# Fused retention and gated feed-forward kernel: the four sums of X move from GpSimd to VectorE, and half of a weight tile is reloaded by two transfers

## Chip, cores and metric

The kernel runs on one core of one Trainium2 chip. The metric is device microseconds of one execution. Time before: median 659.03 us of three runs (656.14 to 660.89).

## What is computed

```python
def _attn_ref(q, k, v):                      # q, k, v: (4, 8, 768, 64) float32
    gamma = 1.0 - 2.0 ** (-5.0 - np.arange(H))
    for t in range(S):
        state = gamma * state + np.einsum('bhd,bhe->bhde', k[:, :, t], v[:, :, t])
        y[:, :, t] = scale * np.einsum('bhd,bhde->bhe', q[:, :, t], state)
...
def _moe_ref(x, w_in, w_out):                # w_in: 512 x 2048, w_out: 2048 x 512
    h = x @ w_in
    g = h * (1.0 / (1.0 + np.exp(-1.702 * h)))
    return g @ w_out
...
    x = attn_out.transpose(0, 2, 1, 3).reshape(B * S, H * D)   # 3072 x 512
```

A recurrence over 768 positions (32 pairs of batch and head) makes X, 3072 rows of 512. X goes through a matrix, a gate and a second matrix.

## The kernel before

The 3072 rows are worked in six blocks of 512 tokens, m = 0 to 5. For each block there is an up part (X times the first matrix, then the gate, into the tile G) and a down part (G times the second matrix, then the output). The retention of the next block (one chunk of 64 positions for two batches at a time, called a step) is interleaved with the down part, so that X of block m+1 is complete when block m's down part is nearly over. Blocks 2 to 5 use a seven-product scheme for both parts: sums and differences of quadrants of the operands are made first, and each 2 by 2 block product then takes seven products instead of eight.

TensorE's order is the program's order. The other engines' orders are decided by a scheduler at build time, except for instructions pinned with `tc.keep_in_program_order`. Each engine works its queue in order: an instruction that waits holds all behind it.

**Sums of X.** The up part of a block reads X as seven pieces. X[:, 0] to X[:, 3] are the quadrants, and `sums_x` (L529 to L533) makes X[:, 4], X[:, 6], X[:, 5] and finally a new X[:, 2] by four subtractions of 128x512 float32 on GpSimd. It is called once a block, in the down part of blocks 1 to 4, after the unit of work that also takes the last retention step (L1025, L1026). Of the four only the first is pinned. `step` (L375) ends with `output` (L338), whose last write of X is the VectorE addition at L352.

**The up part** (`up`, L558) does four groups d, in the order 2, 3, 0, 1 for blocks 3 to 5. In each group the products come in the order P1 (weights in W1A, X[:, 0]), P2 (W1A, X[:, 1]), P6 (weights in LATE, X[:, 5]), P5 (LATE, X[:, 4]), P7 (LATE, X[:, 6]), then P3 and P4 (W1A, X[:, 3] and X[:, 2]). P1, P6, P7 and P4 add up in one PSUM tile, `px`; P2 is in `py`. A product of a group is eight matmuls of 128x256 and about 1.73 us.

**LATE** holds 48 columns of 128 weights per partition. LATE[:, 0:24] serves groups d = 0 and 1, LATE[:, 24:36] serves d = 2 and LATE[:, 36:48] serves d = 3. In the down part the tile is a workspace: `stream` (L651) loads pieces of the second matrix into one quarter and `derive` (L662) has VectorE write sums of G into another. So the weights are reloaded from a copy in HBM, W1D, once a block: ScalarE's queue issues the reload of LATE[:, 24:48] at L766, GpSimd's queue that of LATE[:, 0:24] at L999.

**The down part** (`down49`, L657) has seven products i, each in two halves, so 14 units. L766 stands behind unit i = 5, half 1, the last reader of LATE[:, 24:48]. In blocks 2 to 4 the units of i = 6 follow, whose two halves are in the PSUM tiles `pq` with the tag "x". ScalarE copies each half out (L701, `put`). The first `px` of the next up part takes over the PSUM buffer of the first half, so that TensorE's first matmul of the up part waits for the first of these two copies. Behind them in ScalarE's queue is the copy of P1 out of `px` (L573), which P6 waits for.

**Loads.** SP's queue brings q, k and v for the steps ahead: per step eight transfers each for `q_sq` and `k_sq` (L163), four for `kn_in` and four for `v_in` (L149). As the program is built, every transfer issued from SP's and ScalarE's queues signals its landing on one of eight semaphores, taken in turn; a transfer waits, before it is issued, for the landing of the one that had the same semaphore before it, also where that belongs to the other queue. In block 2 the reload at L766 waits in this way for the third `kn_in` transfer of the step, besides its true dependences (TensorE's last reads, VectorE's L670, an earlier stream and the copy in W1D).

Of the kernel before, what the change touches and what calls it, by code (L numbers as in the profile page):

```python
# [28 lines left out]
def kernel(  # L29
# [29 lines left out]
    pe, act, dve, pool, sp = nc.tensor, nc.scalar, nc.vector, nc.gpsimd, nc.sync  # L59
# [21 lines left out]
    late = ctx.enter_context(tc.tile_pool(name="late", bufs=1))  # L81
# [9 lines left out]
    LATE = late.tile([P, 2 * NP * 3, P], F32, name="LATE")  # L91
    W1L = LATE.rearrange("p (n s c) f -> p n s c f", s=3, c=2)
    W1D = [dram.tile([P, NP * 3, P], F32, name=f"W1D{i}") for i in range(2)]
# [3 lines left out]
    X = const.tile([P, 7, 2, TH], F32, name="X")  # L97
# [428 lines left out]
        pool.tensor_sub(w[5], w[4], w[0])  # L526
        pool.tensor_sub(w[2], w[1], w[5])

    def sums_x():  # L529
        tc.keep_in_program_order(pool.tensor_sub(X[:, 4], X[:, 2], X[:, 0]))  # L530
        pool.tensor_sub(X[:, 6], X[:, 3], X[:, 2])
        pool.tensor_sub(X[:, 5], X[:, 3], X[:, 4])
        pool.tensor_sub(X[:, 2], X[:, 1], X[:, 5])  # L533
# [7 lines left out]
    def sums_w2_t3(p):  # L541
        dve.tensor_sub(W2[:, 6, p:p + 2, :], W2[:, 5, p:p + 2, :], W2[:, 0, p:p + 2, :])
# [92 lines left out]
    def inner_w2_t3(i):  # L635

        b11, b12, b21, b22 = w2q(ORDER[i][1])
        tc.keep_in_program_order(dve.tensor_sub(b12, b22, b12))
# [12 lines left out]
    def stream(i, engine=pool):  # L651

        c = LATE[:, i % 2 * 24:i % 2 * 24 + 12].rearrange("p (k d) e -> p k d e", k=3)
        engine.dma_start(c, W2D[i])  # L654
        return c

    def down49(m, comps):  # L657

        b, t0 = m * CB // NC * 2, m * CB % NC * D
# [4 lines left out]
        def derive(i):  # L664
            q = [G[:, u::2, ORDER[i][0], h * P:(h + 1) * P] for u in range(2) for h in range(2)]
            a11, s3, a12, s2 = q
            d = LATE[:, i % 2 * 24 + 12:i % 2 * 24 + 24].rearrange("p (k d) e -> p k d e", k=3)
            dve.tensor_add(d[:, 0], s2, a11)
            dve.tensor_sub(d[:, 1], a12, s2)
            dve.tensor_add(d[:, 2], s2, s3)  # L670
            b11, t3, b21, b22 = w2q(ORDER[i][1])
            t1, t2, t4 = [comps[i][:, k] for k in range(3)]
            return [(a11, b11), (a12, b21), (s2, t2), (s3, t3)], [(d[:, 0], t1), (d[:, 1], b22), (d[:, 2], t4)]

        def products(p0, pairs, new):
            for j in ((0, 1, 3, 2) if len(pairs) == 4 else range(len(pairs))):
                a, w = pairs[j]
                for d in range(NP // 2):
                    pe.matmul(p0[:, j, :], a[:, d], w[:, d], start=(new and j == 0 and d == 0),  # L679
                              stop=(d == NP // 2 - 1), skip_group_check=True)  # L680
# [33 lines left out]
        def then(i, half, p0):  # L714
            if i == 0:
                act.activation(acc["y", half], p0, AF.Copy)
            elif i == 1:
                put(0, 0, half, p0, None)
            elif i == 2:
                act.activation(keep("u", half), p0, AF.Copy)  # L720
            elif i == 3:
                act.activation(keep("v", half), p0, AF.Copy)
            elif i == 4:
                put(1, 1, half, p0, "v")
            elif i == 5:
                put(0, 1, half, p0, "u")
            else:
                put(1, 0, half, p0, "v" if m == NB - 1 else None)

        def finish(p0, ab):  # L730

            c, v = kept[1, 0], kept["v"][1]
            p1 = ps.tile([P, 2, P], F32, name="pq", tag="x")
            products(p0, ab[:1], True)
            products(p1, ab[1:], True)
            at = [rows[1, 0][:, b, f * P:(f + 1) * P] for b in range(2) for f in range(2)]
            dve.tensor_add(c[:, 1:3], c[:, 1:3], c[:, 0:1].to_broadcast([P, 2, P]))
            act.dma_start(at[0], c[:, 1])
            dve.tensor_add(c[:, 3], c[:, 3], c[:, 2])
            dve.tensor_add(c[:, 4], p0[:, 0], v[:, 0])  # L740
            dve.tensor_add(c[:, 0:5:4], c[:, 2:4], c[:, 4:5].to_broadcast([P, 2, P]))
            act.dma_start(at[3], c[:, 4])
            dve.tensor_add(c[:, 5:7], c[:, 0:4:3], v[:, 1:3])
            dve.tensor_add(c[:, 2:4], p1, c[:, 5:7])
            for n in range(2):
                (act, sp)[n].dma_start(at[1 + n], c[:, 2 + n])
# [3 lines left out]
        for i in range(7):  # L750
            for half in range(2):
                def unit(i=i, half=half):
                    if half == 0:
                        if i == 0:
                            pairs[0] = derive(0)
                        for x in {0: "xy", 4: "y", 6: "y" if m == NB - 1 else ""}.get(i, ""):
                            for n in range(2):
                                acc[x, n] = ps.tile([P, 4 - n, P], F32, name="pq", tag=x)
                    x = "x" if i in (0, 2, 3) or (i == 6 and m < NB - 1) else "y"
                    if i == 6 and half == 1 and m == NB - 1:  # L760
                        finish(acc[x, half], pairs[i][half])
                        return
                    products(acc[x, half], pairs[i][half], i in (0, 4) or (i == 6 and m == NB - 1))
                    then(i, half, acc[x, half])
                    if i == 5 and half == 1 and m < NB - 1:
                        act.dma_start(LATE[:, 24:48], W1D[1])  # L766
                    if half == 0 and i < 6:
                        pairs[i + 1] = derive(i + 1)
                    if half == 1:
                        if i + 2 < 7:  # L770
                            comps[i + 2] = stream(i + 2)
                        if i in (0, 1, 3):
                            sums_g_outer((0, 1, None, 2)[i])
                todo.append(unit)
# [206 lines left out]
    for m in range(NB):  # L981
        between = []
        if m == 0:
            between = [lambda: None, lambda: None, lambda: turn(2 * CB), lambda: step(2 * CB), lambda: None,
                       lambda: turn(2 * CB + 1)]
        elif m == 1:
            between = [lambda: (decay(2 * CB), load(2 * CB + 1, "v"))]
            for j in range(2 * CB + 1, 3 * CB + 1):
                between.append(lambda j=j: (step(j, j - 1), j < 3 * CB and turn(j + 1)))
        elif 1 < m < NB - 1:  # L990
            last = min((m + 2) * CB, NCH - 1)
            for j in range((m + 1) * CB + 1, last + 1):
                between.append(lambda j=j: (step(j, j - 1), j < last and turn(j + 1)))
            if last == NCH - 1:
                between.append(lambda: step(None, NCH - 1))
        if m > 1:
            ds = (0, 1, 2, 3) if m == 2 else (2, 3, 0, 1)
            if m > 2:
                pool.dma_start(LATE[:, 0:24], W1D[0])  # L999
            for n, d in enumerate(ds):  # L1000
                up(d, ds[n - 1] if n else None, ds[n + 1] if n < 3 else None)
                if m == 2 and n < 2:
                    tc.keep_in_program_order(sp.dma_start(W1D[n], LATE[:, 24 * n:24 * n + 24]))
                if n == 0 and m < NB - 1:
                    turn((m + 1) * CB + 1)
                if d == 0:
                    comps = {0: stream(0)}
                if n == 2:
                    comps[1] = stream(1)
                if m == 2:  # L1010
                    for i in range(2 * d, min(7, 2 * d + 2)):
                        inner_w2_t3(i)
        for n, unit in enumerate(down(m) if m < 2 else down49(m, comps)):
            unit()
            if m == 0 and n < NP and n % 2:
                sums_w2(n - 1)
            if m == 0 and NP <= n < 3 * NP // 2:
                sums_w2_t3(2 * (n - NP))
            if m == 1 and n % 8 == 3:
                sums_w1(n // 4)  # L1020
            if (m, n) in INNER:
                inner_w2(INNER.index((m, n)))
            if between and (n in (2, 5, 11, 16, 21) if m == 1 else n % 3 == (1 if m else 2)):
                between.pop(0)()
            if 0 < m < NB - 1 and n == (23 if m == 1 else 11):  # L1025
                sums_x()  # L1026


# [44 lines left out]
```

## Time and profile before

| | before |
|---|---|
| median of three runs | 659.03 us |
| span of the profiled execution | 659.4 us |
| TensorE matmul busy | 639.5 us (97%) |
| VectorE busy | 427.4 us (65%) |
| ScalarE busy | 165.2 us (25%) |
| GpSimd busy | 195.7 us (30%) |
| mean granted TensorE clock | 0.995 |
| LATE<-W1D from ScalarE's queue, 1536 KB, issue to landing | 7.6 us median of 3 |
| LATE<-W2D from GpSimd's queue, 768 KB, issue to landing | 5.0 us median of 28 |
| one subtraction of `sums_x` on GpSimd | 1.27 to 1.28 us |

The profiled execution is one run of the program with the hardware profiler on; no time other than its span is given for it, and the span is 0.4 us above the median of the unprofiled runs. Times in the trace are microseconds from the start of that span. "SPq", "ACTq" and "POOLq" are the queues of SyncE, ScalarE and GpSimd, q1 is the set of DMA rings that SP issues on, q10 those of ScalarE, q0 those of GpSimd. PE is TensorE's matmul, PEld its weight load, DVE is VectorE, ACT is ScalarE and POOL is GpSimd. An idle time is named with what ended it. Block 2's up part runs from 259 to 308 us, its down part to 360; block 3's from 360 to 410 and 462; block 4's from 462 to 512 and 564; block 5 ends the program.

### The profile page before, as it was taken

The numbers are of one execution on the slowest core, as the hardware profiler recorded it, in microseconds if no ns is written. First come the engines' busy times: TensorE is split into PE (matmuls) and PEld (weight loads), VectorE is DVE, ScalarE is ACT, GpSimd is POOL, SyncE is SP. The second block draws the span as 40 slices with busy tenths as digits, with TensorE's granted clock in tenths as the row PEclk, the third lists the DMA queues.
The fourth block names the chain that finished last, engine by engine and source line by source line (L and its number), as shares of the span: only waits on it lengthen the run. The fifth ranks groups of instructions, "written<-read, shape, count | busy, mean of one in ns | idle before, by whom it ended". The sixth has DMA issues, their size and how long they took to land.

```text
span 659.4 us, 15196 instructions
## 1 busy us (share of the span) xinstructions
PE 639.5 (97%) x6390; PEld 577.1 (88%) x6390; DVE 427.4 (65%) x599; ACT 165.2 (25%) x320; POOL 195.7 (30%) x222
## 2 busy tenths in 40 slices
PE   6789999999999999999999999999999999999997
PEld 3678888888788888889999888999888999888997
DVE  3699989999936963348883336984145984144855
ACT  4674334551000000333101323100333210233210
POOL 6400321210478218000727400535500335500000
PEclk9799999999999999999999999999999999999999
DMA  9996649763243456550577821486741244601142
GB/s 174 185 274 186 175 89 246 188 139 54 48 96 144 120 155 160 183 169 1 157 161 213 224 50 49 124 192 175 235 79 49 71 141 145 237 2 49 52 157 97
DMA packets 148149, 89.77 MB, mean 136 GB/s; under 512 B 131600, under 2 KB 134416, under 8 KB 147056
## 3 DMA queue, kind: packets, MB, share of 16 engines
q1 hardware_dynamic: 135856, 44.66, 30.2%
q0 software_dynamic: 9456, 38.16, 18.5%
q10 hardware_dynamic: 2768, 5.96, 2.6%
q8 instruction: 50, 0.82, 0.5%
q14 instruction: 19, 0.16, 0.1%
HBM read 71.32 MB, written 14.94 MB: 131 GB/s over the span
## 4 chain that ended last, share of the span: by engine, by line
PE 83%; DMA 8%; DVE 4%; SPq 2%; POOL 1%; issue 1%; ACT 0%; DVEq 0%; ACTq 0%; POOLq 0%
PE pq L679 22%; PE px L564 16%; PE pd L814 13%; PE pz L564 8%; PE ph L417 8%; PE ph L492 7%; PE py L564 4%; DMA W<-in_moe_w_in_dram 2%; PE pa L294 2%; DMA LATE<-W1D 1%; DMA G<-in_moe_w_in_dram 1%; PE py L317 1%; PE py L311 1%; PE pa L302 1%; DMA kn_in<-in_k_dram 1%; SPq L146 1%
## 5 line engine op out<-in xcount | busy, mean ns | idle before, releaser
L654 POOL DMA_DIRECT2D LATE<-W2D x28 | 15.5, 555 | 236.4 <-PE pq L679 125.0
L679 PE MATMUL pq<-W,G 128*128 128x128 f32 x672 | 80.2, 276 | 0.0
L679 PEld LDWEIGHTS pq<-W,G 128*128 128x128 f32 x672 | 77.6, 192 | 0.6
L564 PE MATMUL px<-X,LATE 128*128 128x256 f32 x256 | 60.7, 380 | 2.2 <-DMA LATE<-W1D 1.2
L564 PE MATMUL px<-X,W1A 128*128 128x256 f32 x256 | 60.5, 379 | 0.0
L679 PE MATMUL pq<-LATE 128*128 128x128 f32 x448 | 59.8, 276 | 0.0
L417 PE MATMUL ph<-X,W1A 128*128 128x256 f32 x256 | 57.4, 382 | 1.6 <-DVE X L352 1.1
L564 PEld LDWEIGHTS px<-X,LATE 128*128 128x128 f32 x256 | 48.5, 190 | 9.5 <-issue 1.5
L417 PEld LDWEIGHTS ph<-X,W1A 128*128 128x128 f32 x256 | 48.0, 190 | 8.5 <-DVE X L352 1.2
L679 PEld LDWEIGHTS pq<-LATE 128*128 128x128 f32 x448 | 54.5, 192 | 0.4
L564 PEld LDWEIGHTS px<-X,W1A 128*128 128x128 f32 x256 | 48.4, 190 | 6.5
L814 PE MATMUL pd<-W,G 128*128 128x256 f32 x224 | 49.6, 381 | 0.0
L814 PEld LDWEIGHTS pd<-W,G 128*128 128x128 f32 x224 | 42.2, 190 | 5.8
L599 DVE TENSOR_TENSOR G<-pz,vv 128x512 f32<-128x512 f32 x16 | 11.1, 692 | 49.3 <-ACT vv L579 49.3
L398 ACT ACTIVATE G<-G 128x512 f32<-128x512 f32 x48 | 29.8, 628 | 44.4 <-DVE G L607 22.2
L814 PE MATMUL pd<-W,LATE 128*128 128x256 f32 x160 | 35.8, 382 | 1.2 <-DVE LATE L548 1.2
L814 PEld LDWEIGHTS pd<-W,LATE 128*128 128x128 f32 x160 | 30.1, 190 | 6.2 <-DVE LATE L548 2.2
L701 ACT ACTIVATE o<-pq 128x512 f32<-128x512 f32 (+1 forms) x14 | 7.6, 544 | 90.8 <-PE pq L679 90.8
L564 PE MATMUL pz<-X,W1A 128*128 128x256 f32 x128 | 30.3, 379 | 0.0
L564 PE MATMUL py<-X,W1A 128*128 128x256 f32 x128 | 30.2, 379 | 0.0
L564 PE MATMUL pz<-X,LATE 128*128 128x256 f32 x128 | 30.2, 379 | 0.0
L679 PE MATMUL pq<-LATE,G 128*128 128x128 f32 x224 | 29.6, 275 | 0.0
(206 smaller groups left out, 1175.3 us busy)
## 6 DMA issues: line engine op xcount, KB each, us to landing
LATE<-W2D POOLq DMA_DIRECT2D x28, 768.0 KB, 5.0
W<-in_moe_w_in_dram SPq DMA_DIRECT2D x12, 512.0 KB, 4.8
W<-in_moe_w_out_dram SPq DMA_DIRECT2D x10, 512.0 KB, 5.0
out_dram<-o POOLq DMA_DIRECT2D x20, 256.0 KB, 3.8
q_sq<-in_q_dram SPq DMA_DIRECT2D x144, 32.0 KB, 2.5
k_sq<-in_k_dram SPq DMA_DIRECT2D x144, 32.0 KB, 2.2
v_in<-in_v_dram SPq DMA_DIRECT2D x72, 64.0 KB, 3.0
LATE<-W1D ACTq DMA_DIRECT2D x3, 1536.0 KB, 7.6
```

The lines of the kernel that those rows point to most:

```text
L146: keep(engine.dma_start(*((to, at) if name == "v" else (to[:, n:H:2], at[:, n * HP:(n + 1) * HP]))))
L294: pe.matmul(pa[HALF[w], u, 0, s, :], kt[HALF[u], w, s, :], qt[HALF[u], w, s, :], start=True, stop=True)
L302: pe.matmul(pa[HALF[u], w, 1, s, :], kd[HALF[w], HP * u + s, :], vn[HALF[w], HP * u + s, :], start=True, stop=True)
L398: pin(act.activation(g, h[:, i], AF.Gelu_apprx_sigmoid))
L417: pe.matmul(h[:, ab], w, X[:, 2 * th + c // 2, c % 2, :], start=(ab == 0 and c == 0), stop=(c == 3), skip_group_check=True)
L492: pe.matmul(acc[:, u, :], w, x, start=(start and u == 0 and c == 0), stop=(stop and c == 1), skip_group_check=True)
L564: pe.matmul(acc[:, u, :], w1(2 * d + u, sw)[:, c, :], X[:, sx, c, :], start=(start and u == 0 and c == 0), stop=(stop and c == 1), skip_gr ...
L599: dve.tensor_add(a[3], z, v)
L654: engine.dma_start(c, W2D[i])
L679: pe.matmul(p0[:, j, :], a[:, d], w[:, d], start=(new and j == 0 and d == 0), stop=(d == NP // 2 - 1), skip_group_check=True)
L701: act.activation(to, y, AF.Copy)
L814: pe.matmul(p0[:, n, :], g1(m, p, sa)[:, n * P:(n + 1) * P], W2[:, sb, p, :], start=(new and p == 0 and n == 0), stop=(last and p == NP - ...
```

## The change

For blocks 2 to 4 (`m > 1`) the four subtractions are done by VectorE, in the order X[:, 4], X[:, 5], X[:, 6], X[:, 2], all four pinned. In VectorE's order as built they stand behind the last step's L352 and the copy-out of unit i = 5 (L703), and ahead of the first addition of the next up part (L588). Block 1 keeps GpSimd. The reload of LATE[:, 24:48] becomes two transfers, of LATE[:, 24:36] and of LATE[:, 36:48], both from ScalarE's queue at the same place. TensorE's order does not change; lines after the edits are 4 or 5 higher in the changed kernel.

```diff
-    def sums_x():
+    def sums_x(late):
+        if late:
+            for to, a, b in ((4, 2, 0), (5, 3, 4), (6, 3, 2), (2, 1, 5)):
+                tc.keep_in_program_order(dve.tensor_sub(X[:, to], X[:, a], X[:, b]))
+            return
         tc.keep_in_program_order(pool.tensor_sub(X[:, 4], X[:, 2], X[:, 0]))
         pool.tensor_sub(X[:, 6], X[:, 3], X[:, 2])
         pool.tensor_sub(X[:, 5], X[:, 3], X[:, 4])
...
                     if i == 5 and half == 1 and m < NB - 1:
-                        act.dma_start(LATE[:, 24:48], W1D[1])
+                        for a in range(2):
+                            act.dma_start(LATE[:, 24 + 12 * a:36 + 12 * a], W1D[1][:, 12 * a:12 * a + 12])
...
             if 0 < m < NB - 1 and n == (23 if m == 1 else 11):
-                sums_x()
+                sums_x(m > 1)
```

## The prediction

> **What bounds the kernel now.** I read the page's busy times and chain of waits first, then who TensorE waits for, then the timeline at the three places that the change touches: the passages from a down part to the next up part near 360, 462 and 564 us.
>
> ```profile
> PE 639.5 (97%) x6390; PEld 577.1 (88%) x6390; DVE 427.4 (65%) x599; ACT 165.2 (25%) x320; POOL 195.7 (30%) x222
> ```
>
> The first line is busy us, share and instructions of each engine; the next two are TensorE's waits, with the total, the count and the longest in us.
>
> ```profile
> PE px L564 <- DMA LATE<-W1D: 1.2, 1, 1.2
> PE px L564 <- POOL X L532: 1.0, 1, 1.0
> ```
>
> TensorE is busy 97% of the span, so only what it waits for can pay, and the change can remove two of these waits, one each. The third passage (564 us) has no wait at all. The first passage, block 2 to 3, in the timeline (start, duration, engine, line):
>
> ```profile
> 355.19 2.57 SPq L149 DMA_DIRECT2D v_in<-in_v_dram  x4
> ...
> 356.44 0.36 ACTq L766 DMA_DIRECT2D LATE<-W1D  x1
> ...
> 357.41 0.60 ACT L701 ACTIVATE o<-pq 128x512 f32<-128x512 f32 x1 [20.08 <-PE pq L679]
> ...
> 359.84 1.89 PE L564 MATMUL px<-X,W1A 128*128 128x256 f32 x8
> ...
> 363.17 1.27 POOL L532 TENSOR_TENSOR X<-X 128x512 f32<-128x512 f32 x1
> ...
> 364.49 1.99 PE L564 MATMUL px<-X,LATE 128*128 128x256 f32 x8 [1.03 <-POOL X L532]
> ```
>
> P1 starts at 359.84, P2 1.73 later; P6 could start at 359.84 + 2 x 1.73 = 363.30 and starts at 364.49, when GpSimd has made X[:, 5]: a loss of 1.19. Right behind that wait is another: the reload of LATE, issued at 356.44, takes 7.6 and so lands at 364.0. The sums alone, moved, would gain only 0.45. The second passage:
>
> ```profile
> 457.50 0.33 ACTq L766 DMA_DIRECT2D LATE<-W1D  x1
> ...
> 459.92 0.60 ACT L701 ACTIVATE o<-pq 128x512 f32<-128x512 f32 x1 [20.27 <-PE pq L679]
> ...
> 467.12 1.97 PE L564 MATMUL px<-X,LATE 128*128 128x256 f32 x8 [1.16 <-DMA LATE<-W1D]
> ```
>
> P1 starts at 462.35 and P2 at 464.07, so P6 could start at 465.80: a loss of 1.32, to the reload. X[:, 5] is ready at 466.0 there. Both parts of the change are needed to win anything in full, and all there is to win is 1.19 + 1.32 = 2.5 us.
>
> **The sums, on VectorE.** Removed: 12 subtractions of 1.27 us from GpSimd, 15.2 us of a queue that is 30% busy. The output sums, output transfers and the reload of LATE[:, 0:24] behind them come up to 5 us earlier; that reload is first read some 24 us later (group 0 is third), so the gain there is nothing. Added: 12 to VectorE at 0.69 us (rows of 128x512 without PSUM, such as L615, mean 692 ns), 4 x 0.72 with the start gaps, so 2.9 us a block. VectorE is free: in block 2 its L703 ends at 354.35 and its next instruction, L588, starts at 363.57 after 9.22 us idle. The sums run from 354.4 to 357.3; X[:, 5] is there 6 us before 363.3. If GpSimd works at the same time, VectorE's 128x512 rows reach 1.4 to 1.5 us (L668 and L669 near 344 us); even then the sums end at 360.5. Cost nothing, and the cover is 6 us. In block 3 L703 ends at 456.85, sums end at 459.8 to 463, against 465.8.
>
> **The first half of the reload.** 768 KB instead of 1536 KB from the same issue time. The nearest rows are the 28 stream loads of 768 KB into LATE: 4.5 us at the least, 5.0 in the median, 6.5 in the worst that did not share with L999. I take 5.0: it lands at 361.4 in block 2 and 462.5 in block 3, ahead of 363.3 and 465.8 by 1.9 and 3.3. Even 6.5 gives 362.9 and 464.0. The reload's wait goes in both.
>
> **The second half, and what it holds.** In the built program the second transfer takes the next free semaphore, and that is one that SP's queue used last. In block 2 it waits for the landing of the third v_in transfer of the step, in block 3 for the fourth, in block 4 for one some 30 us old. The wait stands in ScalarE's queue, and behind it stand both copies L701 and the copy L573. TensorE's P1 needs the first L701 for its PSUM buffer. So when the third v_in lands decides when block 3 starts.
>
> The four v_in of block 2 are issued from 355.19 on, about 0.65 apart, the third at 356.5, just behind the reload. How long it takes, SP's queue tells: its sixth q_sq waits for the same semaphore.
>
> ```profile
> SPq L163 <- DMA v_in<-in_v_dram: 3.2, 1, 3.2
> ```
> ```profile
> q10 hardware_dynamic: 87, 1.07, 92.8%
> q1 hardware_dynamic: 44, 0.01, 1.6%
> ```
>
> The first line is SP's waits from 355 to 366 us; the five q_sq before it went out by 361, and 3.2 later is 364.2. The others (queue, packets, MB, share of the engines' time) are the DMA queues from 358.5 to 361.5: ScalarE's reload has the engines, and SP's loads get 1.6%. So the third v_in landed at 364.2, 0.2 behind the reload. With half the reload ahead of it, it lands 0.2 behind that half: 356.44 + 5.0 + 0.2 = 361.6 (361.1 with 4.5, 363.1 with 6.5). Then the issue (0.36), a start gap (0.1), L701 (0.60) and the release of TensorE (0.05, as from L532 to P6): P1 at 362.7 instead of 359.84, P6 at 362.7 + 3.46 = 366.2. All else that P6 needs is there. Against 364.49 that is a loss of 1.7 (1.2 to 3.2).
>
> The Trainium skill, "DMA: Bandwidth & Descriptors", section "Anatomy of one DMA", gives about 2.0 us fixed per transfer plus bytes over 436 GB/s, fitted on GpSimd's path, which speaks against splitting and would make the half 3.8 us. By it the third v_in lands at 360.4, P1 starts at 361.5, and block 2 loses 0.5 instead of 1.7.
>
> In block 3 the fourth v_in is issued at 456.57, 0.9 before the reload, and lands 3.4 later, at 460.0. The first L701 there is due at 459.92 and would end at about 461.1; P1 is due at 462.35. 1.2 us of cover, so nothing is lost, and the 1.32 is won. In block 4 nothing waits before or after. SP's own waits on the two halves delay q_sq and k_sq by an estimated 2 us at most (a second half issued at 361.6 that takes as long as the whole did, 7.6, against 367.6 before); block 2's are read near 417 us.
>
> Sum: 1.7 - 1.3 = +0.4 on 659.4. The three runs' median lies 0.4 below the profiled span, so I predict 659.03 + 0.4 = 659.4.
>
> **The clock.** A 2.9 us idle TensorE is longer than any pause after 22 us. What a pause can do shows at the start:
>
> ```profile
> 16.20:19.40 3.20, 1.16 (x64) 1.05 (x64) 0.77 (x2) 1.04 (x2) 3.20 (x6) 1.00 1.13 158
> 19.50:22.80 3.30, 1.38 (x34) 1.29 (x35) 1.91 (x4) 3.00 (x9) 2.48 (x5) 0.50 0.99 279
> 22.90:26.20 3.30, 3.30 (x76) 2.97 (x78) 2.79 (x5) 1.20 (x2) 1.24 (x3) 0.50 1.24 192
> ```
>
> The third column is TensorE's busy time, the third from the end the granted clock. After a stretch that was 36% busy, in which a pause of 3.53 us began, it was 0.50 for 6.8 us. At 36 us a pause of 1.5 left it at 1.00. The price is between nothing and 3.4 us (6.8 at half rate); full work stands on both sides of the new pause, unlike there, so I take nothing as likeliest, but only just. The skill's "TensorE: Matmul & The Clock Gate", section "Part 1: The HAM clock gate", puts the drop after an idle window of about 3.4 us; by it 2.9 us would cost nothing, while the rows show the drop 1.5 us into the pause.
>
> **Rivals.** (1) Faster: the third v_in gets through beside the half reload and ScalarE is hardly held. Below a landing at 359.9 block 2 gains (P1 at 361.0, P6 at 364.5 as before); from 358.7 down L701 ends by 359.8 and both waits go in full, 659.03 - 2.5 = 656.5. With v_in's median, 3.0 us, it lands at 359.5, P6 comes 0.4 earlier than before, and the sum is -1.7: 657.3. For it: that median, and the fourth v_in of block 3 at 3.4 us. Against: the 1.6% above. (2) Slower: the hold in block 2 lasts as long as the worst stream row, 6.5 us, and the clock drops. P6 is then 3.2 late, minus 1.3, plus 1.7 for one stretch of 3.4 at half rate to 3.4 for two: 662.6 to 664.3. It decides where TensorE's pause passes about 3 us, that is a v_in later than 361.7. (3) The sums on VectorE come too late or hold L588: with 6 us of cover, no; I give it nothing.
>
> **The numbers.** Forecast 0.50, rival 1 0.22, rival 2 0.28. The three runs before spread over 4.8 us, and a median of so few can miss by one; 656.0 to 663.0 takes in rival 1 and the lower part of rival 2. About 1% (6.6 us) is what a measurement of this kernel can tell from no change: below 652.4 there is no mechanism (0.03), above 665.6 only rival 2 with both its prices high (0.05), within 0.92.
>
> **What would show it.** In the profile of the changed kernel: P6 of block 3 (px<-X,LATE) no longer ended by L532 nor by LATE<-W1D; four VectorE subtractions from about 354.4; a gap of 2 to 4 us before the first px of block 3, ended by ACT L701 (its new number 705); ScalarE's second reload issue 4 to 6 us after its first; no gap at the block 4 passage. If the two issues stand together in block 2, my step on the semaphore is wrong and rival 1 holds. A granted clock below 1 near 365 us is rival 2.

## Result and profile after

The changed kernel takes 666.25 us (median of 14 runs, 661.83 to 669.0) against 659.53 us before (median of 14, 656.14 to 664.24). The medians differ by 6.7 us. The ratio is 1.0081, 95% interval 1.0056 to 1.0106; it is taken over the runs and not of the two medians, and makes the loss 5.3 us. The prediction was 659.4 us, +0.4, and its range ended at 663.0.

From the page of the changed kernel: busy time by engine, the granted clock in 40 slices, the chain of waits by engine, and the group of P1's matmuls (busy us, mean ns, idle time before them and what ended it).

```profile
PE 641.7 (96%) x6390; PEld 578.6 (87%) x6390; DVE 437.7 (66%) x611; ACT 165.2 (25%) x320; POOL 182.2 (27%) x210
...
PEclk9899999999999999999998999999899999999999
...
PE 84%; DMA 8%; DVE 4%; SPq 2%; ACT 1%; issue 0%; ACTq 0%; DVEq 0%
...
L568 PE MATMUL px<-X,W1A 128*128 128x256 f32 x256 | 63.9, 395 | 5.9 <-ACT o L705 5.9
```

The same row of the clock and the same group of P1's matmuls from the page of the kernel before:

```profile
PEclk9799999999999999999999999999999999999999
...
L564 PE MATMUL px<-X,W1A 128*128 128x256 f32 x256 | 60.5, 379 | 0.0
```

TensorE's two waits at P6 (1.0 for L532, 1.2 for LATE<-W1D) are gone, and P1 now waits 5.9 us in two places for ScalarE's copy L705 (L701 before). Two 8s stand in the clock row that the row before has not, near 365 and 470 us. P1's group is 3.4 us busier with the same 256 matmuls (60.5 before): that is the clock. The passage from block 2 to 3 in the timeline (start, duration, engine, line):

```profile
354.74 1.27 SPq L149 DMA_DIRECT2D v_in<-in_v_dram  x2
...
354.80 0.69 DVE L532 TENSOR_TENSOR X<-X 128x512 f32<-128x512 f32 x1
...
355.14 5.67 ACTq L771 DMA_DIRECT2D LATE<-W1D  x2
...
361.07 0.98 ACT L705 ACTIVATE o<-pq 128x512 f32<-128x512 f32 x2 [25.26 <-DMA v_in<-in_v_dram]
...
361.72 3.63 PE L568 MATMUL px<-X,W1A 128*128 128x256 f32 x8 [3.21 <-ACT o L705]
...
365.18 1.89 PE L568 MATMUL py<-X,W1A 128*128 128x256 f32 x8
...
366.91 1.89 PE L568 MATMUL px<-X,LATE 128*128 128x256 f32 x8
```

The sums end at 355.5, eleven us before P6 starts. ScalarE's two issues span 5.67 us: the second goes out at 360.49, when the third v_in (issued 354.74) has landed at 360.41. Only then come the copies, and TensorE has paused 3.21 us when P1 starts. P1 itself takes 3.63 us where a product took 1.89. The same in front of block 4, SP's and ScalarE's rows of the timeline:

```profile
457.55 3.53 SPq L149 DMA_DIRECT2D v_in<-in_v_dram  x4
...
459.34 7.35 ACTq L771 DMA_DIRECT2D LATE<-W1D  x2
...
466.89 0.98 ACT L705 ACTIVATE o<-pq 128x512 f32<-128x512 f32 x2 [24.93 <-DMA q_sq<-in_q_dram]
```

The first half landed at 465.88, the fourth v_in, issued at 459.51 just behind it, at 466.23, and the second half went out at 466.32. (The profile puts L705's idle time down to a q_sq that landed at 466.39; by the semaphores it is the fourth v_in.) P1 starts after 2.72 us of pause.

The granted clock in the trace changes only on a grid of 3.413 us, from 1.00 to 0.50 or back. In the steps of that grid (start:end, length, busy time of each engine, then granted clock, DMA share, GB/s):

```profile
358.23:361.65 3.42, 0.27 (x3) 0.08 (x1) 0.00 (x0) 0.58 (x2) 0.75 (x1) 1.00 1.17 271
361.65:365.06 3.41, 3.34 (x8) 2.72 (x9) 0.00 (x0) 0.40 (x2) 3.07 (x5) 0.50 1.04 274
365.06:368.47 3.41, 3.41 (x18) 3.00 (x17) 0.69 (x1) 1.16 (x2) 0.88 (x2) 1.00 0.93 296
...
464.05:467.46 3.41, 0.77 (x7) 0.58 (x6) 0.00 (x0) 0.57 (x2) 1.07 (x2) 1.00 0.56 129
467.46:470.87 3.41, 3.33 (x8) 2.70 (x9) 0.00 (x0) 0.41 (x2) 3.06 (x5) 0.50 0.98 271
```

A step in which TensorE (first figure) was busy 0.27 or 0.77 us is followed by one at 0.50, which costs half its length, 1.7 us.

The two profiled spans, 659.4 and 665.4, can be put side by side from the first P1 of one block to that of the next. P1 of blocks 2 to 5 starts at 259.29, 359.84, 462.35 and 563.83 us before, and at 257.77, 361.72, 467.54 and 569.35 after:

| stretch | before | after | difference |
|---|---|---|---|
| start to P1 of block 2 | 259.3 | 257.8 | -1.5, ahead of the change: one clock step at the start instead of two |
| P1 of block 2 to P1 of block 3 | 100.55 | 103.95 | +3.4, the hold |
| block 3 to block 4 | 102.51 | 105.82 | +3.3: first clock step +1.7, wait at P6 gone -1.2, second hold +2.8 |
| block 4 to block 5 | 101.48 | 101.81 | +0.3: second clock step +1.7, wait at P6 gone -1.3 |
| block 5 | 95.57 | 96.05 | +0.5 |

So the waits that the change was to remove did go, 2.5 us, and two holds (6.2 us) and two clock steps (3.4 us) took their place. Over all runs the clock's part is smaller: the mean granted clock of the 14 runs is 0.9931, which is 4.6 us lost at half rate, against 2.6 us in the 55 runs of the kernel before that the experiments below ran beside: 2.0 us of the loss.

### The profile page after: what moved, and what is told of

It is laid out like the page before. It is cut to its first block, busy times and chain, and to the rows that moved or that the text cites. A ratio compares the mean times of both kernels' runs of the same rounds, so it can differ in the third digit from the quotient of the medians.

```text
span 665.4 us, 15197 instructions
## 1 busy us (share of the span) xinstructions
PE 641.7 (96%) x6390; PEld 578.6 (87%) x6390; DVE 437.7 (66%) x611; ACT 165.2 (25%) x320; POOL 182.2 (27%) x210
## 4 chain that ended last, share of the span: by engine, by line
PE 84%; DMA 8%; DVE 4%; SPq 2%; ACT 1%; issue 0%; ACTq 0%; DVEq 0%
PE pq L683 22%; PE px L568 17%; PE pd L819 13%; PE pz L568 8%; PE ph L417 7%; PE ph L492 7%; PE py L568 4%; DMA v_in<-in_v_dram 3%; DMA W<-in_moe_w_in_dram 2%; DMA k_sq<-in_k_dram 2%; PE pa L294 2%; DMA G<-in_moe_w_in_dram 1%; PE py L317 1%; PE py L311 1%; PE pa L302 1%; SPq L146 1%
## 5 line engine op out<-in xcount | busy, mean ns | idle before, releaser
L568 PE MATMUL px<-X,W1A 128*128 128x256 f32 x256 | 63.9, 395 | 5.9 <-ACT o L705 5.9
L568 PEld LDWEIGHTS px<-X,W1A 128*128 128x128 f32 x256 | 50.6, 199 | 13.5 <-ACT o L705 6.3
L568 PE MATMUL px<-X,LATE 128*128 128x256 f32 x256 | 60.5, 379 | 0.0
L705 ACT ACTIVATE o<-pq 128x512 f32<-128x512 f32 (+1 forms) x14 | 7.4, 543 | 96.3 <-PE pq L683 27.0
```

Source lines behind the costliest of these rows:

```text
L568: pe.matmul(acc[:, u, :], w1(2 * d + u, sw)[:, c, :], X[:, sx, c, :], start=(start and u == 0 and c == 0), stop=(stop and c == 1), skip_gr ...
L705: act.activation(to, y, AF.Copy)
```

## Experiments

Theory A: the loss comes from the wait that the second transfer takes in ScalarE's queue, in two blocks, with the clock behind it. Rivals: the moved sums cost; the split or its volume costs; the clock is no part of the price. Each ratio is to runs of the kernel before from the same time, with medians of 659.58 (sums alone, split alone, second half later, second half from GpSimd), 661.26 (tiny transfer, three quarters, first filler, block 3 only) and 659.24 (short filler, more lead).

**Sums alone.** The change with one whole reload:

```diff
-                        for a in range(2):
-                            act.dma_start(LATE[:, 24 + 12 * a:36 + 12 * a], W1D[1][:, 12 * a:12 * a + 12])
+                        act.dma_start(LATE[:, 24:48], W1D[1])
```

> Only the first half of the change: the sums of blocks 2 to 4 on VectorE, the reload of LATE[:, 24:48] as one transfer. Theory A (the loss is ScalarE's queue held by the second transfer, 3.2 and 2.7 us, plus a clock drop behind each pause, about 1.7 us each): no hold here, P6 of block 3 waits for the reload in place of the sums, 0.4 us gained; -0.5 us against before (ratio 0.999), no clock drop after 30 us. Rival B (the moved sums, or GpSimd's work and the reload of LATE[:, 0:24] coming earlier, make the loads late): +5 us (ratio 1.008).

Measured: 659.98, ratio 1.0004 (0.9985 to 1.0023). One wait over 0.5 us is left behind 200 us:

```profile
365.96 1.97 PE L568 MATMUL px<-X,LATE 128*128 128x256 f32 x8 [0.77 <-DMA LATE<-W1D]
```

P6 of block 3 waits for the reload in place of the sums, as the prediction read from the landing at 364.0. The moved sums cost nothing that shows; the interval ends at 1.5 us.

**Split alone.** The sums stay on GpSimd, two transfers:

```diff
-    def sums_x(late):
-        if late:
-            ...
+    def sums_x():
...
-                sums_x(m > 1)
+                sums_x()
```

> Only the second half of the change: the sums stay on GpSimd, the reload is split as in the change. Theory A: the same two holds and clock drops as in the changed kernel, P1 of blocks 3 and 4 waits for ScalarE's copy for about 3 us each; +5 to +7 us (ratio 1.008 to 1.011). Rival B: the split alone only removes block 3 to 4's reload wait, -1.3 us (ratio 0.998).

Measured: 666.45, ratio 1.0097 (1.0061 to 1.0133): the split alone carries the whole loss. P1 waits 1.87 us in front of block 3 and 2.11 in front of block 4. Two steps of the grid around the first:

```profile
359.16:362.58 3.42, 1.55 (x13) 1.34 (x12) 0.00 (x0) 0.98 (x2) 2.96 (x4) 1.00 1.01 241
362.58:365.99 3.41, 3.41 (x10) 2.69 (x9) 0.00 (x0) 0.33 (x1) 3.25 (x4) 0.50 0.96 284
```

A pause of 1.87 us, all of it within one step, is enough for the drop.

**Second half later on the same queue.** It is pinned behind the copy of P1 (L577) and the first gate of the next block:

```diff
-                        for a in range(2):
-                            act.dma_start(LATE[:, 24 + 12 * a:36 + 12 * a], W1D[1][:, 12 * a:12 * a + 12])
+                        act.dma_start(LATE[:, 24:36], W1D[1][:, 0:12])
...
+        if more:
+            more()
         product(x, d, "P6", False, False)
...
-                up(d, ds[n - 1] if n else None, ds[n + 1] if n < 3 else None)
+                up(d, ds[n - 1] if n else None, ds[n + 1] if n < 3 else None,
+                   (lambda: tc.keep_in_program_order(act.dma_start(LATE[:, 36:48], W1D[1][:, 12:24]))) if m > 2 and n == 0 else None)
```

> The change, with the second half's transfer issued behind the copy of P1 (L577) and the first gate of the next up part, so that whatever it waits for, the two copies of pq and that of P1 are ahead of it in ScalarE's queue. Theory A: both holds, both clock drops and both old waits go, -2.5 us against before (ratio 0.996), P1 of block 3 starts at its time; if the new place waits for SP's k_sq it holds the next copy (u) by up to 1 us. Rival C (two transfers in place of one are slow in themselves, by their sharing of the engines with SP's loads): P6 of blocks 3 and 4 still waits for LATE<-W1D, no gain or a loss (ratio 1.000 or more).

Measured: 672.89, ratio 1.0177 (1.0136 to 1.0219), the opposite of what was expected. P1 came on time, but the wait went with the transfer. ScalarE's rows:

```profile
362.85 0.63 ACT L398 ACTIVATE G<-G 128x512 f32<-128x512 f32 x1 [1.87 <-DVE G L592]
369.40 0.33 ACTq L1008 DMA_DIRECT2D LATE<-W1D  x1
369.78 0.60 ACT L583 ACTIVATE u<-px 128x512 f32<-128x512 f32 x1 [6.30 <-DMA k_sq<-in_k_dram]
```

At the new place the transfer waits for a k_sq that went out shortly before it, and behind it stands the copy L583, for which TensorE paused 4.96 and 5.56 us, with 6.8 us at 0.50 each time. The expectation had named a k_sq at the new place, at up to 1 us; this one went out at 362.36 and took 7.0. A transfer issued later has a later one ahead of it on its semaphore, and what that one takes was not looked at.

**Second half from GpSimd's queue.** Same program place, same volume:

```diff
-                            act.dma_start(LATE[:, 24 + 12 * a:36 + 12 * a], W1D[1][:, 12 * a:12 * a + 12])
+                            (act, pool)[a].dma_start(LATE[:, 24 + 12 * a:36 + 12 * a], W1D[1][:, 12 * a:12 * a + 12])
```

> The change, with the second half's transfer issued from GpSimd's queue at the same point of the program: no semaphore shared with SP's loads, both halves in flight together. Theory A: no hold of ScalarE, no clock drop; the first half shares the engines and lands between 5.0 and 7.6 us after its issue, so P6 of block 3 waits 0 to 0.7; -1.5 to -2.5 us against before (ratio 0.996 to 0.998). Rival C: as slow as the change, because the second transfer in flight delays the first and SP's loads as much (ratio 1.005 or more).

Measured: 658.49, ratio 0.998 (0.9962 to 0.9998). It is the only version here under both kernels. In the timeline of the passage from block 2 to 3:

```profile
355.35 0.35 ACTq L771 DMA_DIRECT2D LATE<-W1D  x1
...
356.26 0.60 ACT L705 ACTIVATE o<-pq 128x512 f32<-128x512 f32 x1 [20.08 <-PE pq L683]
...
356.95 0.56 POOL L771 DMA_DIRECT2D LATE<-W1D  x1
...
358.69 1.89 PE L568 MATMUL px<-X,W1A 128*128 128x256 f32 x8
...
362.14 1.89 PE L568 MATMUL px<-X,LATE 128*128 128x256 f32 x8
```

L705 follows the first issue at once, P1 and P6 come without any wait, and the clock stays at 1.00 from 30 us to the end. SP's third v_in landed as late as in the changed kernel, 5.7 us after its issue, so that a late load costs nothing by itself: here no issue of ScalarE's waited for it. The median gained is 1.1 us of the 2.5 that the two waits were worth; the interval holds both 0.2 and 3.8 thousandths.

**A tiny second transfer in the kernel before.** The whole reload and GpSimd's sums stay; one transfer of 8 KB that nobody reads goes out behind the reload on ScalarE's queue:

```diff
+    TINY = dram.tile([P, 16], F32, name="TINY")
...
                         act.dma_start(LATE[:, 24:48], W1D[1])
+                        act.dma_start(TINY, kept[0, 1][:, 6, 0:16])
```

> The kernel before, sums on GpSimd and one whole reload of 1536 KB, with one transfer of 8 KB that nobody reads (128x16 float32 to HBM) behind the reload in ScalarE's queue. Theory A (what costs is the wait that a second transfer on this queue takes with its semaphore, whatever it moves): ScalarE is held until a load of SP lands that went out near the whole reload, which takes 7.6 us; the first copy of the unit behind it comes 3 to 6 us late, TensorE pauses before the first P1 of blocks 3 and 4, the granted clock drops behind it, ratio 1.010 to 1.020. Rival (the volume of the second half, or splitting the reload, is what costs): 8 KB cost nothing, ratio 0.998 to 1.002.

Measured: 675.28, ratio 1.0206 (1.0169 to 1.0243), at the upper end of theory A's range. ScalarE's rows in front of block 3:

```profile
354.44 0.35 ACTq L767 DMA_DIRECT2D LATE<-W1D  x1
362.58 0.34 ACTq L768 DMA_DIRECT2D TINY<-o  x1
363.12 0.98 ACT L702 ACTIVATE o<-pq 128x512 f32<-128x512 f32 x2 [28.29 <-DMA q_sq<-in_q_dram]
```

8 KB held the queue for 7.8 us, until a q_sq landed behind the reload, and TensorE paused 6.26 and 3.92 us. With the previous run this settles it from both sides: the second 768 KB without the wait on this queue cost nothing, and the wait with 8 KB in place of them costs 14 us, here behind the whole reload.

**Three quarters first.** The change split 18 to 6 columns:

```diff
-                        for a in range(2):
-                            act.dma_start(LATE[:, 24 + 12 * a:36 + 12 * a], W1D[1][:, 12 * a:12 * a + 12])
+                        act.dma_start(LATE[:, 24:42], W1D[1][:, 0:18])
+                        act.dma_start(LATE[:, 42:48], W1D[1][:, 18:24])
```

> The change with the reload split 18 to 6 columns of 128 instead of 12 to 12: the first transfer is 1152 KB, the second 384 KB. Theory A (ScalarE's second transfer waits for a small load of SP that does not get through until the transfer ahead of it has landed): the first transfer takes 6.5 to 8 us instead of 5.6 and 6.5, each hold grows by about that difference, TensorE's pauses before P1 become 4 to 5 us, the clock drops for 3.4 to 6.8 us behind each, ratio 1.010 to 1.017. Rival (two transfers share the engines and P6 starves): the order of sizes matters little, pauses as in the change, ratio 1.008 to 1.010.

Measured: 672.26, ratio 1.0149 (1.011 to 1.0187), inside theory A's ratio. TensorE waits 5.53 and 5.48 us before P1, more than the 4 to 5 expected: the hold grows with the transfer ahead. Part of that is another small load: here the second transfer waits in block 2 for the fourth v_in and in block 3 for a q_sq.

**Filler in the pauses.** The change with TensorE work between the last unit of blocks 2 and 3 and P1, first six matmuls written, then three (each is run on the chip as two of 0.43 us):

```diff
+            if 2 < m < NB - 1:
+                warm = ps_a.tile([P, 2, 2, HP, D], F32, name="warm", tag="pa")
+                for n in range(6):
+                    pe.matmul(warm[:, 0].rearrange("p a h t -> p (a h t)"), ident, W2[:, 0, 0:2].rearrange("p a e -> p (a e)"),
+                              start=True, stop=True)
```

> The change with six added matmuls of 128x512 (float32, about 0.43 us each, 2.6 us in all, their output not used) on TensorE between the last down unit of blocks 2 and 3 and the first P1 of the next block. They need nothing that ScalarE's queue holds, so they stand in the two pauses of 3.2 and 2.7 us. Theory A (the loss is two pauses and, behind each, 3.4 us at a granted clock of 0.50): the holds stay, what is left of each pause is under 0.7 us, the granted clock stays at 1.00, and 2 x 1.7 = 3.4 us of the change's loss go: a ratio of about 1.003 to before instead of 1.008 to 1.010. Rival (the clock record is not what costs, or the drop has another cause than the pause): the drop stays or its going changes nothing, 1.008 or more.

> The change with added TensorE work of half the length of the first filler: in each of the two pauses 2.6 us (six matmuls on the chip, of 0.43 us each, where the first filler had twelve and 5.3 us, longer than the hold). Theory A: the hold of ScalarE's queue is as in the change, what is left of the pauses of 3.2 and 2.7 us is under 1 us, the granted clock stays at 1.00 behind 30 us, and against the change's span of 665.4 us the 2 x 1.7 us of the clock go: a span of about 662, ratio 1.002 to 1.005. Rival (the clock is not a part of the price): the drop stays without the pause, or its going changes nothing, ratio 1.008 or more.

Measured: 670.08, ratio 1.013 (1.0103 to 1.0157), and 664.94, ratio 1.0079 (1.0052 to 1.0107). The first was twice as long as meant, so it outlasts the hold: by its row below P1 comes 5.3 us late in both blocks whatever ScalarE does, and 2 x 5.3 - 2.5 = 8.1 is what it should cost; 8.8 were measured. It says nothing on the size of the hold.

```profile
359.60 5.32 PE L1008 MATMUL warm<-W,UB 128*128 128x512 f32 x12
364.75 1.46 PE L568 MATMUL px<-X,W1A 128*128 128x256 f32 x6
```

In both kernels the clock stays at 1.00 behind 26 us: no pause, no drop. But the second did not give back the 3.4 us: it is 1.3 us below the changed kernel, with overlapping intervals, and its ratio lies where the rival had it and not at theory A's 1.002 to 1.005. Its mean clock over 7 runs is 0.9963, 2.5 us lost instead of 4.6; part of that went into the filler, since each passage now costs the longer of filler and hold. In its profile block 2 was not held at all (the second half went out at 358.70) and still paid 2.6 us. So that the drop hangs on the pause is shown; its price is read from the records (1.7 us a step), and these times do not show it.

**Split in block 3 only.**

```diff
-                        for a in range(2):
-                            act.dma_start(LATE[:, 24 + 12 * a:36 + 12 * a], W1D[1][:, 12 * a:12 * a + 12])
+                        if m == 3:
+                            for a in range(2):
+                                act.dma_start(LATE[:, 24 + 12 * a:36 + 12 * a], W1D[1][:, 12 * a:12 * a + 12])
+                        else:
+                            act.dma_start(LATE[:, 24:48], W1D[1])
```

> The change with two transfers only in block 3; blocks 2 and 4 reload with one, all sums on VectorE as in the change. In block 3 the second half waits for the fourth v_in, as in the change. Theory A1 (block 3's hold came from the disturbance in block 2, which let SP's fourth v_in go out 0.17 us behind the reload instead of 0.9 us ahead): the fourth v_in is ahead of the reload again, lands within 3.5 us, no pause in front of block 4, no clock drop anywhere after 30 us, P6 of block 4 waits for nothing, ratio 0.997 to 0.999. Rival A2 (the load starves behind the half reload whether it is issued just ahead of it or just behind): a pause of 2 to 3 us in front of block 4 and 3.4 us at 0.50 behind it, ratio 1.004 to 1.005.

Measured: 663.23, ratio 1.0027 (0.9998 to 1.0055), between the two. The profile shows a hold, as A2 has it:

```profile
455.07 7.72 ACTq L772 DMA_DIRECT2D LATE<-W1D  x2
462.99 0.98 ACT L705 ACTIVATE o<-pq 128x512 f32<-128x512 f32 x2 [25.36 <-DMA q_sq<-in_q_dram]
```

The fourth v_in went out at 454.64, 0.43 ahead of the half reload, and landed at 462.35, behind the reload's 462.18. (L705's idle time is put down to a q_sq here too; the second half went out at 462.43, when the fourth v_in had landed.) Block 2 was undisturbed (P1 and P6 without a wait), and still the lead of 0.9 us did not come back and block 3 was held, with a pause of 3.11 us. Block 3's hold does not need one in block 2.

**More lead for the small load.** Seven copies in place were to put the reload of block 2 off:

```diff
+                        for n in range({2: 7}.get(m, 0)):
+                            tc.keep_in_program_order(act.activation(acc[x, half], acc[x, half], AF.Copy))
                         for a in range(2):
```

> The change with seven copies of 128x384 in place (0.5 us each, values unchanged) on ScalarE ahead of the two transfers in block 2 alone. They put the first half off from 355.1 to about 356.5 us, so that SP's third v_in, on which the second half waits, goes out some 1.5 us ahead of it instead of 0.4. Nothing else is moved; block 3 is as in the change. Theory A (whether the small load gets through is decided by how far it goes out ahead of the half reload: with 0.9 us and more it lands 3.4 to 3.9 us after its issue, with 0.55 and less only when the reload has landed): in block 2 the second half goes out by 359, the pause in front of block 3 is 1.2 us or less, no clock drop behind it; block 3 keeps its pause of 2 to 3 us and its drop; ratio 1.001 to 1.004. Rival (the load is starved by the half reload whichever goes first): the second half goes out at 362, the pause in front of block 3 is 4 us or more with a drop behind it, ratio 1.009 to 1.012.

Measured: 665.81, ratio 1.0084 (1.0056 to 1.0113). The edit did not do what it was for. ScalarE's rows:

```profile
354.89 0.36 ACTq L773 DMA_DIRECT2D LATE<-W1D  x1
355.35 0.47 ACT L771 ACTIVATE pq<-pq 128x384 f32<-128x384 f32 x1 [19.20 <-DVE X L532]
357.77 0.33 ACTq L773 DMA_DIRECT2D LATE<-W1D  x1
358.14 0.47 ACT L771 ACTIVATE pq<-pq 128x384 f32<-128x384 f32 x1 [2.32 <-DMA v_in<-in_v_dram]
358.53 0.59 ACT L705 ACTIVATE o<-pq 128x512 f32<-128x512 f32 x1
```

The scheduler set the copies behind the first issue, so the reload was not put off. The run is of use in another way. In this execution the third v_in, only 0.29 ahead of the reload, landed 3.1 us after its issue, block 2 was not held, and the time was 660.72, the lowest of its nine runs. In the split-alone kernel the same load with the same lead of 0.29 took 5.3 us. So the lead alone does not settle whether the small load gets through.

## Why the prediction was wrong

- **"1.2 us of cover, so nothing is lost"** (block 3) is the first step that failed, and it brought block 3 from -1.3 to +3.2 us (+2.8 hold, +1.7 clock, -1.3). The cover stood on one number, that the fourth v_in went out 0.9 us ahead of the reload. Nothing fixes that lead: the two go out from different queues, each when what it waits for is there. In the changed kernel it was -0.17 us, and v_in took 6.7 us instead of 3.4. The v_in next to ScalarE's first reload in blocks 2 and 3 of all twelve traces show what a lead is worth. All 25 that went out 0.93 to 1.6 us ahead of it landed 2.3 to 4.0 us after their issue. Of 22 with leads of 0.30 to 0.87 six landed 1.7 to 4.2 us ahead of the reload, and 16 no earlier than 0.8 us ahead of it. The 21 with less lead, or behind it, all landed after it. Two with a lead of 0.87, one of block 3 in the kernel with more lead, one in that with the tiny transfer:

```profile
L149 SPq DMA_DIRECT2D v_in<-in_v_dram x1: 614/614/614, 454.9 to 454.9; - x1
DMA to landing us min/median/max: 6.5/6.5/6.5
...
L150 SPq DMA_DIRECT2D v_in<-in_v_dram x1: 622/622/622, 461.0 to 461.0; - x1
DMA to landing us min/median/max: 3.9/3.9/3.9
```

So the 0.93 of the kernel before was the least of the leads that always sufficed, with nothing to spare. These are rows of executions as they came; no experiment set the lead.
- **The clock, "nothing as likeliest, but only just"**, is the second. It dropped after both holds: 3.4 us in the profile, 2.0 in the mean over the runs. The row of the start of the program, a drop 1.5 us into a pause, was the better guide than the thought that full work on both sides would help (in the step of the grid before that drop, 16.02 to 19.44 us, TensorE was idle for 2.25 us in all). The Trainium skill, "TensorE: Matmul & The Clock Gate", section "Part 1: The HAM clock gate", describes a free-running activity window of 3413 ns and a drop after an idle window of about 3.4 us. The grid is in every trace here; that the window must be idle is not borne out. In the twelve traces, behind 30 us and ahead of the last steps of the programs, eleven drops follow a step with 1.87 us or more of idle TensorE, and no step at 1.00 with 1.83 or less is followed by one.
- **Block 2's hold** was right in kind and size: the pause was to be 2.9 us and was 3.2, without the clock P6 came 2.2 us later where 1.7 (1.2 to 3.2) was written. The first half took 5.6 us rather than 5.0, and 6.5 in block 3; SP's loads took 54.1% of the DMA engines' time from 358.3 to 361 us, not 1.6% as beside the whole reload. The estimate from the skill's figures, 3.8 us by "DMA: Bandwidth & Descriptors", section "Anatomy of one DMA", was further off.
- **The sums** cost nothing that shows and **both waits at P6** went, as written (the first experiment; rival 3 rightly had no chance). The four ran from 352.8 to 355.5.
- **Rivals.** The way it went is that of rival 2, and its point (a pause past about 3 us) was passed in block 2. Its price was too low, 662.6 to 664.3, because it let block 3 gain. It was written for a first half of 6.5 us; in block 2 5.6 were enough for the drop.
- **Span and median.** The sum was made against a span of 659.4, said to be 0.4 above the median. A run's time is 1.7 us above its span here (667.08 and 665.4 for the profiled run of the changed kernel), so that profiled execution was an estimated 661.1, 1.6 above the median of 659.53. It moved no term.

It stays open why, of two loads with the same lead, one gets through and the other does not.

## What to carry to other kernels

Before a second transfer is put on a queue, find out which landing its issue waits for and who stands behind it there; from GpSimd's queue, where it had no such wait, the same 768 KB cost nothing. A lead or slack between two queues that a single execution shows is no cover, since it changed here with the edits: the fourth v_in of block 3 went out 0.93 us ahead of the reload, 0.17 behind it and 0.43 ahead in three of these kernels. A new pause of TensorE cost its length here, and from about 1.85 us on up to another 1.7 us for each clock step.

## What was not expected of the hardware

In these traces the drop of the clock goes by TensorE's idle time within a fixed step of 3.413 us and not by the length of a pause. So a pause between 1.87 and some 3.7 us (an estimate: twice 1.85) may or may not cause it, by where it lies. A pause of 1.86 us that began in one step and ended in the next left the clock at 1.00 (the kernel with more lead, in front of block 4):

```profile
458.03:461.45 3.42, 2.98 (x27) 2.79 (x25) 1.92 (x2) 0.00 (x0) 3.04 (x4) 1.00 0.79 216
461.45:464.86 3.41, 1.99 (x9) 1.78 (x10) 0.00 (x0) 0.98 (x2) 1.97 (x5) 1.00 0.82 230
464.86:468.27 3.41, 3.41 (x18) 3.00 (x17) 0.69 (x1) 1.23 (x2) 2.15 (x3) 1.00 1.17 283
```

And in the kernel split 18 to 6 the step with 1.83 us of idle time is still followed by one at 1.00, the step after it, wholly idle, by 0.50:

```profile
468.57:471.98 3.41, 1.58 (x15) 1.39 (x13) 0.00 (x0) 0.00 (x0) 1.50 (x3) 1.00 0.92 283
471.98:475.40 3.42, 0.00 (x0) 0.00 (x0) 0.00 (x0) 0.41 (x1) 0.00 (x0) 1.00 0.20 35
475.40:478.81 3.41, 3.17 (x8) 2.55 (x9) 0.00 (x0) 0.56 (x2) 2.90 (x5) 0.50 0.87 185
```
